# Eight products and no sums in the first pass of a seven-product kernel, with the first tiles placed between products

## The chip, the cores and the metric

The kernel runs on one core of a Trainium2 chip. The metric is the device time in microseconds (us). The engines are PE (TensorE: matmuls and transposes), DVE (VectorE), ACT (ScalarE), POOL (GpSimd) and SP (SyncE, which issues the DMAs here); each works through its own queue in order.

## The reference

Attention over chunks of 64 tokens, then two feed-forward layers, all in 32-bit floats:

```python
def _attn_ref(q, k, v):                       # q, k, v: (4, 8, 576, 64)
    ...
    scores = scale * np.matmul(q_c, k_c.transpose(0, 1, 2, 4, 3))
    scores = scores - np.max(scores, axis=-1, keepdims=True)
    attn = np.exp(scores)
    attn = attn / (np.sum(attn, axis=-1, keepdims=True) + 1e-09)
    out = np.matmul(attn, v_c)

def _moe_ref(x, w_in, w_out):                 # x: (2304, 512), w_in: (512, 2048)
    h = x @ w_in
    g = h * (1.0 / (1.0 + np.exp(-1.702 * h)))
    return g @ w_out

def _moe2_ref(x, w_in, w_out):
    h = x @ w_in
    sp = np.where(h > 20.0, h, np.log1p(np.exp(np.minimum(h, 20.0))))
    g = h * np.tanh(sp)
    return g @ w_out
```

The weights arrive as 64-bit floats.

## The kernel before

**Passes, blocks, steps.** Each layer's hidden dimension is cut in two, so there are four passes (n = 0 to 3; 0 and 1 are the first layer). A pass goes over five blocks of tokens: block 0 has 256 tokens, blocks 1 to 4 have 512 each; the order is 1, 0, 2, 3, 4 in the first three passes. A block has four steps (p = 0 to 3), each over two groups of 128 hidden rows. So there are 80 steps, numbered through: 0 to 3 are block 1 of the first pass, 4 to 7 block 0, 8 to 19 blocks 2 to 4; step 20 begins the second pass.

**A step** (`run`, from L539) makes the hidden rows of its two groups, applies the activation, and between its products runs the four `filler`s, which are the output products of the step before. Every value is kept as a high part (`fp32r`) and the rest, and a product of two values is three matmuls (`mm3`, L361); a product of one step's quarter is six matmuls of 256 columns (`prod`, L366). A *direct* step (`s.direct`) makes its 2 x 2 quarters with eight such products, in `half(h, c)`. The other steps make them with seven products of sums: four operands of weights (`S1` to `S4`, built by `Weights.add`) and four of tokens (`T1` to `T4`, built by `sums_of_tokens`); the running product X is copied out three times by ACT (`snap`, L611, L616, L622), and DVE adds three times (L617, L626, L638). In such a step the activation of the second half (L639) is asked for at the end of the step. `parts_before` makes high part and rest of that half (L381, L89) in the next step. Direct before the change are block 0 of every pass, and block 1 of the first pass. Steps before `FREE` write only to the PSUM banks x and y; from then on every second step uses a0 and a1.

**Preparation of operands.** `split` casts a quarter of tokens to a high part (ACT, L243) and subtracts for the rest (DVE); a seven-product block needs seven such splits, a direct one four. The buffers have names (`tag`) from B11 to T4. A weight piece (`pieces0`) arrives as pairs of 32-bit words; `convert` does scale (ACT, L130), join (DVE, L136 and L137), cast (ACT, L155) and rest (DVE, or POOL for the output weights). In the first pass the sums of weights come last: `sums_of_first` rebuilds the weights from their parts (L166, POOL and DVE) and adds, in steps 4 to 7.

**Attention** works on 18 tiles of 128 tokens (`Attention`). A tile is: two transposes (q, k) with a copy each by ACT, scores (L301), maximum and difference on DVE, exp on ACT, sums on DVE, normalising on POOL (L326), a transpose (L334) with a copy by ACT, and two products with the values (L347) with copies by DVE. Tiles 0 and 1 come before step 0, tiles 2 and 3 in `second_half`, which step 0 runs after its first two products. The others are cut into *ticks* (`ticks_of`), spread over the steps by `done` (27 of them in steps 0 to 3, all within steps 0 to 14). Each step has nine places (`place(0)` to `place(8)`) at which generators that have begun go on by one piece (`go_on`), and new ones begin. What is emitted there stands in that order in every engine's queue.

## Time and profile before

| | us |
|---|---|
| median of 3 runs | 938.03 (937.55 to 938.88) |
| the profiled execution | 935.45 |
| its span | 933.7 |
| PE busy | 871.1 (93%) |
| DVE busy | 589.6 (63%) |
| ACT busy | 398.4 (43%) |
| POOL busy | 71.8 (8%) |

All times of the trace are of the profiled execution, in us from the start of its span. Busy time of PE has modelled ends: consecutive matmuls overlap, and what one costs is read from start to start. The granted clock is a share of 2.4 GHz; 0.5 is 1.2 GHz. The steps start at: 0: 23.68, 1: 63.91, 2: 83.80, 3: 99.40, 4: 116.74, 7: 149.46, 8: 167.73, 9: 184.99, 15: 281.85, 19: 324.16, 20: 336.41.

### The profile page before, as it was taken

The page shows a single profiled execution, that of the slowest core. Times are in us where ns is not written, and L with a number is a line of the kernel's source. Part 1 is how long each engine was busy: PE and PEld are TensorE (multiplying, and loading weights), DVE is VectorE, ACT ScalarE, POOL GpSimd, SP SyncE. Part 2 cuts the span into 40 slices and gives each one's busy share as a digit, 9 for nine tenths or more (in the row PEclk, how much of TensorE's full clock was granted, in tenths as well). Part 3 has the DMA queues.
Part 4 walks back from the last instruction along what each step waited for, and adds up shares of the span by engine and source line. Part 5 has one row for each costly group of instructions (what it writes and reads, how often), then busy time and mean ns, then how long its engine had stood idle before and what let it go on. Part 6 is the DMA issues. An engine that isn't in the chain of part 4 may idle for free.

```text
span 933.7 us, 16021 instructions
## 1 busy us (share of the span) xinstructions
PE 871.1 (93%) x6318; PEld 776.9 (83%) x6318; DVE 589.6 (63%) x1121; ACT 398.4 (43%) x799; POOL 71.8 (8%) x60
## 2 busy tenths in 40 slices
PE   6679997789989988999999999999999999999998
PEld 4567777777879877998999989889999889999987
DVE  4456567546557888867767876545556785546442
ACT  3356564544545464443435444323243553323220
POOL 1011221000000111000000021000001110000000
PEclk9769998999999999999999999999999999999999
DMA  9464543233236667786767531210204242030202
GB/s 226 154 152 119 119 114 80 62 64 91 58 114 240 212 216 270 242 298 220 237 220 252 176 119 40 91 68 1 91 26 156 81 146 102 34 113 1 92 18 73
DMA packets 112491, 121.10 MB, mean 130 GB/s; under 512 B 60960, under 2 KB 80928, under 8 KB 110368
## 3 DMA queue, kind: packets, MB, share of 16 engines
q1 hardware_dynamic: 112416, 120.08, 41.2%
q8 instruction: 49, 0.80, 0.3%
q14 instruction: 26, 0.21, 0.1%
HBM read 83.89 MB, written 36.18 MB: 129 GB/s over the span
## 4 chain that ended last, share of the span: by engine, by line
PE 50%; DVE 4%; DMA 2%; ACT 1%; issue 1%; SPq 0%; ACTq 0%; DVEq 0%
PE acc L416 7%; PE acc L417 7%; PE acc L418 7%; PE x L362 4%; PE x L364 4%; PE x L363 4%; PE y L364 3%; PE y L363 3%; PE y L362 3%; PE acc L362 2%; PE acc L363 2%; PE acc L364 2%; DMA raw2o<-in_moe_w_out_dram 1%; DMA raw2i<-in_moe_w_in_dram 0%; DVE T1p L89 0%
## 5 line engine op out<-in xcount | busy, mean ns | idle before, releaser
L362 PE MATMUL acc<-gh,wo 128*128 128x512 f32 (+1 forms) x320 | 123.5, 386 | 0.0
L363 PE MATMUL acc<-gl,wo 128*128 128x512 f32 (+1 forms) x320 | 119.2, 372 | 0.0
L364 PE MATMUL acc<-gh,wo 128*128 128x512 f32 (+1 forms) x320 | 118.1, 369 | 0.0
L416 PE MATMUL acc<-wo,gh 128*128 128x512 f32 x288 | 113.8, 395 | 0.0
L417 PE MATMUL acc<-wo,gh 128*128 128x512 f32 x288 | 113.7, 395 | 0.0
L418 PE MATMUL acc<-wo,gl 128*128 128x512 f32 x288 | 112.0, 389 | 0.0
L381 DVE CAST gh<-t 128x512 fp32r<-128x512 f32 (+1 forms) x160 | 68.9, 430 | 67.9 <-ACT t L639 34.6
L89 DVE TENSOR_TENSOR gl<-t,gh 128x512 fp32r<-128x512 f32 (+1 forms) x160 | 105.7, 661 | 6.3
L639 ACT ACTIVATE t<-t 128x512 f32<-128x512 f32 x60 | 37.9, 632 | 130.3 <-DVE t L638 130.3
L364 PEld LDWEIGHTS acc<-gh,wo 128*128 128x128 f32 x320 | 60.5, 189 | 11.1
L362 PEld LDWEIGHTS acc<-gh,wo 128*128 128x128 f32 x320 | 60.9, 190 | 7.6
L363 PEld LDWEIGHTS acc<-gl,wo 128*128 128x128 f32 x320 | 60.9, 190 | 5.4
L418 PEld LDWEIGHTS acc<-wo,gl 128*128 128x128 f32 x288 | 54.1, 188 | 12.3
L416 PEld LDWEIGHTS acc<-wo,gh 128*128 128x128 f32 x288 | 54.6, 190 | 7.0
L417 PEld LDWEIGHTS acc<-wo,gh 128*128 128x128 f32 x288 | 54.7, 190 | 6.1
L626 DVE TENSOR_TENSOR t<-y,snap 128x256 f32<-128x256 f32 x60 | 25.3, 422 | 50.4 <-ACT snap L622 50.1
L616 ACT COPY snap<-x 128x256 f32<-128x256 f32 x60 | 22.3, 372 | 77.8 <-PE x L364 77.8
L622 ACT COPY snap<-x 128x256 f32<-128x256 f32 x60 | 22.3, 372 | 74.2 <-PE x L364 74.0
L301 PE MATMUL sc<-kt,qt 64*64 64x64 f32 x576 | 23.7, 240 | 22.5 <-ACT kt L290 20.4
L362 PE MATMUL x<-T2p,ws 128*128 128x256 f32 x120 | 35.4, 295 | 9.3 <-ACT snap L611 9.2
L301 PEld LDWEIGHTS sc<-kt,qt 64*64 64x64 f32 x576 | 21.1, 152 | 27.1 <-ACT kt L290 24.0
L632 ACT ACTIVATE t<-x 128x256 f32<-128x256 f32 x60 | 23.0, 383 | 47.6 <-PE x L364 47.5
(715 smaller groups left out, 2403.2 us busy)
## 6 DMA issues: line engine op xcount, KB each, us to landing
x<-x SPq DMA_DIRECT2D x16, 1024.0 KB, 6.1
part<-ps SPq DMA_DIRECT2D x34, 256.0 KB, 2.4
pl<-part SPq DMA_DIRECT2D x34, 256.0 KB, 4.4
out_dram<-pl SPq DMA_DIRECT2D x18, 256.0 KB, 2.1
v<-in_v_dram SPq DMA_DIRECT2D x16, 256.0 KB, 5.3
raw1i<-in_moe_w_in_dram SPq DMA_DIRECT2D x8, 512.0 KB, 5.2
raw1o<-in_moe_w_out_dram SPq DMA_DIRECT2D x8, 512.0 KB, 4.3
raw2i<-in_moe_w_in_dram SPq DMA_DIRECT2D x8, 512.0 KB, 4.4
```

The source lines that it names most:

```text
L89: eng.tensor_tensor(out=o, in0=a, in1=b, op=ALU.subtract)
L301: nc.tensor.matmul(pt[rs, o : o + CH], self.qt[rs, c0 : c0 + CH], self.kt[rs, c0 : c0 + CH], start=True, stop=True,)
L362: nc.tensor.matmul(o, wh, mh, start=start, stop=False, skip_group_check=more)
L363: nc.tensor.matmul(o, wh, ml, start=False, stop=False, skip_group_check=more)
L364: nc.tensor.matmul(o, wl, mh, start=False, stop=stop, skip_group_check=more)
L381: vec(gh[s, f][:, :n], t[:, :n])
L416: nc.tensor.matmul(o, a[:, ts], wh, start=start, stop=False)
L417: nc.tensor.matmul(o, a[:, ts], wl, start=False, stop=False)
L418: nc.tensor.matmul(o, b[:, ts], wh, start=False, stop=stop)
L626: nc.vector.tensor_add(tb[:, HB:], Y, snap[2])
L632: nc.scalar.activation(ta[:, HB:], X, func)
L639: nc.scalar.activation(tb, tb, func)
```

## The change

All blocks of the first pass are direct: eight products a step, no `snap`, no sums of tokens, no sums of weights (`rebuild` and `sums_of_first` go). The tokens of blocks 0, 2, 3 and 4 are split when half a block and the whole block have come (`TWO`, `MORE`, with buffers that are free then). The seven parts for the first seven-product block, in step 20, are made in step 19 (`AFTER_PASS`). `second_half` gets the products as its argument: tile 2's transposes and scores come ahead of the first product, tile 3's ahead of the second; weight pieces 2 to 4 are converted in it. Step 0 has no ticks any more; the ticks are spread over steps 1 to 15, 21 of them in steps 1 to 3, and `FREE` is 16. `load_next` loads one piece at each conversion, and pieces from 11 on use the first pieces' rooms again. In a seven-product step the activation of the second half is asked for in the next step (`act_before`), behind the first snapshot (or, in a direct step, behind the first half-product), and `parts_before` stands behind the first addition.

```diff
@@ -159,13 +160,6 @@
             both = self.parts[kind, f]
             sub(eng, both[:, 1], self.f32[kind, f], both[:, 0].bitcast(F32))
 
-        def rebuild(self, kind, f, eng):
-
-            t = wf32.tile([P, DM], F32, tag="wf", name=f"wr{self.n}{kind}{f}")
-            both = self.parts[kind, f].bitcast(F32)
-            eng.tensor_tensor(out=t, in0=both[:, 0], in1=both[:, 1], op=ALU.add)
-            self.f32[kind, f] = t
-
         def add(self, p):
 
             a, b = self.f32["i", 2 * p], self.f32["i", 2 * p + 1]
@@ -373,7 +367,7 @@
             mm3(o, wh[:, ws], wl[:, ws], mh, ml, start and kk == 0, stop and kk == 1, more)
 
     gh, gl = {}, {}
-    func = [AF.Gelu_apprx_sigmoid, AF.Mish]
+    func_of = lambda s: (AF.Gelu_apprx_sigmoid, AF.Mish)[s.m]
 
     def parts_of_g(s, f, t, n):
         gh[s, f] = gp.tile([P, 2 * HB], F32R, tag="gh", name=f"gh{s}{f}")
@@ -386,7 +380,7 @@
 
         def __init__(self, s, n, j, p):
             self.s, self.n, self.m, self.j, self.p = s, n, n // 2, j, p
-            self.direct = j == 0 or (n == 0 and j == 1)
+            self.direct = j == 0 or n == 0
             self.cols = size[j]
 
         def fillers(self):
@@ -485,7 +479,7 @@
         live, shifted = {}, []
         EARLY, SLOTS = 4, 8
 
-        FREE = 15
+        FREE = 16
 
         def go_on():
             for todo in list(going):
@@ -544,7 +538,7 @@
 
         def run(s, prev, jobs, middle=None):
 
-            p, w, func = s.p, W[s.n], (AF.Gelu_apprx_sigmoid, AF.Mish)[s.m]
+            p, w, func = s.p, W[s.n], func_of(s)
             fill = prev.fillers() if prev else [lambda: None] * 4
             n = s.cols
             tx, ty = ("a0", "a1") if s.s >= FREE and s.s % 2 else ("x", "y")
@@ -564,6 +558,11 @@
                         begin(todo())
                     del queue[:k]
 
+            def act_before():
+                for _, _, t, n in pending:
+                    nc.scalar.activation(t[:, :n], t[:, :n], func_of(prev))
+                exps()
+
             def parts_before():
                 while pending:
                     parts_of_g(*pending.pop(0))
@@ -578,13 +577,14 @@
                     prod(oc, w.operand(p, f"A{h + 1}2"), rhs[c][1], False, True)
 
                 if middle:
-                    half(0, 0)
-                    half(1, 0)
-                    middle()
+                    middle(half)
                 for h in range(2):
                     for c in range(1 if middle else 0, len(rhs)):
                         half(h, c)
-                        parts_before()
+                        if (h, c) == (0, 0):
+                            if prev and not prev.direct:
+                                act_before()
+                            parts_before()
                         place(4 * h + c)
                     t = tp.tile([P, 2 * HB], F32, tag=f"t{h}", name=f"t{s.s}{h}")
                     filler(2 * h)
@@ -610,11 +610,13 @@
                 prod(V, w.operand(p, "A12"), "B21")
                 act(snap[0], X)
                 prod(Y, w.operand(p, "S3"), "T3")
-                parts_before()
+                if prev and not prev.direct:
+                    act_before()
                 place(0)
                 prod(X, w.operand(p, "S2"), "T2", start=False, more=True)
                 act(snap[1], X)
                 nc.vector.tensor_add(ta[:, :HB], V, snap[0])
+                parts_before()
                 place(1)
                 filler(0)
                 place(2)
@@ -636,8 +638,6 @@
                 place(7)
                 filler(3)
                 nc.vector.tensor_add(tb[:, :HB], Y, snap[1])
-                nc.scalar.activation(tb, tb, func)
-                exps()
                 pending.append((s.s, 1, tb, n))
                 place(8)
             for h in range(2):
@@ -646,21 +646,26 @@
 
 
         w0 = W[0]
-        spare = []
-        for i in range(4):
-            t = wres.tile([P, 2, DM, 2], I32, tag=f"ws{i}", name=f"early{i}")
-            spare += [t[:, 0], t[:, 1]]
+        def early():
+
+            while True:
+                for i in range(4):
+                    t = wres.tile([P, 2, DM, 2], I32, tag=f"ws{i}", name=f"early{i}")
+                    yield t[:, 0]
+                    yield t[:, 1]
+
+        spare = early()
         pieces0 = [("i", 0), ("i", 1)]
         for p in range(NQ):
             if p + 1 < NQ:
                 pieces0 += [("i", 2 * p + 2), ("i", 2 * p + 3)]
             pieces0 += [("o", 2 * p), ("o", 2 * p + 1)]
-        loading, loaded = iter(pieces0), [0]
+        loading = iter(enumerate(pieces0))
 
         def load_next():
-            if (key := next(loading, None)) is not None:
-                w0.load(*key, room=spare.pop(0) if spare else None)
-                loaded[0] += 1
+            c, key = next(loading, (0, None))
+            if key:
+                w0.load(*key, room=next(spare) if c < 8 or c > 10 else None)
 
         for i in range(EARLY):
             live[i] = Attention(i)
@@ -717,22 +722,38 @@
         for f in range(2):
             w0.drop("i", f)
 
-        def second_half():
-
-            for a in (a2, a3):
-                whole(a.turn("q", "a0", act))
-                whole(a.turn("k", "a1", act))
-                whole(a.scores("o0" if a is a2 else "o1"))
-                a.exp()
-                a.sums(nc.gpsimd)
+        def second_half(half):
+
+            whole(a2.turn("q", "a0", act))
+            whole(a2.turn("k", "a1", act))
+            whole(a2.scores("o0"))
+            begin(convert(2))
+            half(0, 0)
+            a2.exp()
+            go_on()
+            whole(a3.turn("q", "a0", act))
+            whole(a3.turn("k", "a1", act))
+            whole(a3.scores("o1"))
+            a2.sums(nc.gpsimd)
+            begin(convert(3))
+            go_on()
+            half(1, 0)
+            a3.exp()
+            go_on()
+            whole(a2.turn_e("a0", act))
+            a3.sums(nc.gpsimd)
             tile_of(4)
-            whole(a2.turn_e("a0", act))
-            whole(a3.turn_e("a1", act))
+            go_on()
             whole(a2.values(0, "o2", vec))
             whole(a2.values(1, "o3", vec))
+            go_on()
+            begin(convert(4))
+            whole(a3.turn_e("a1", act))
+            go_on()
             whole(a3.values(0, "a0", vec))
-            whole(a3.values(1, "a1", vec))
+            whole(a3.values(1, "o0", vec))
             split_now(1, {"B12": "T1", "B22": None}, cols)
+            go_on()
             keep(0, 1)
 
         def convert(c):
@@ -741,19 +762,12 @@
             w0.scale(kind, f)
             yield
             w0.join(kind, f)
-            while loaded[0] < min(c + 7, len(pieces0)) and (loaded[0] < 11 or loaded[0] - 3 <= c):
-                load_next()
+            load_next()
             yield
             w0.cast(kind, f)
             yield
             w0.rest(kind, f, nc.vector if kind == "i" else nc.gpsimd)
             w0.drop(kind, f)
-
-        def sums_of_first(p):
-            w0.rebuild("i", 2 * p, nc.gpsimd)
-            w0.rebuild("i", 2 * p + 1, nc.vector)
-            yield
-            yield from w0.add(p)
 
         def rooms(kind, w, p):
 
@@ -810,35 +824,34 @@
                 source[c] = quarter(xs[0, j], c)
                 yield from split(c, to, tag)
 
-        marks = []
+
+        TWO = {0: {"B11": "T2", "B21": "T3"}, 2: {"B11": "T4", "B21": "B11"}}
+        TWO |= {3: {"B11": "B22", "B21": "T2"}, 4: {"B11": None, "B21": None}}
+        MORE = {2: {"B12": "B21", "B22": "T1"}, 3: {"B12": "T3", "B22": "T4"}}
+        MORE |= {4: {"B12": "T1", "B22": None}}
         for i in range(EARLY, NTILE + 1):
             ticks += ticks_of(i)
-            if i == 6:
-                ticks.append(lambda: now(lambda: keep(0, 0)))
-                ticks.append(lambda: splits(0, {"B11": "T2", "B21": "T3"}, fresh))
-            elif i == 8:
-                ticks.append(lambda: splits(2, {"B11": None, "B21": None}, fresh))
-            elif i > 8 and i % 4 == 2:
-                j = place(i - 1)[0]
+            j, t = place(i - 1)
+            if t == 1 and j != 1:
+                ticks.append(lambda j=j: splits(j, TWO[j], fresh))
+            if t == 3 and j != 1:
+                ticks.append(lambda j=j: splits(j, MORE[j], fresh))
+            if (t + 1) * P == size[j] and j != 1:
                 ticks.append(lambda j=j: now(lambda: keep(0, j)))
-                ticks.append(lambda j=j: sums_of_tokens(0, j))
-                ticks += [lambda: now(lambda: None)] * 3
-                if i == 10:
-                    ticks += [lambda c=c: split(c, fresh) for c in ("B22", "T1", "T4")]
-                marks.append(len(ticks))
-
-        half = marks[0] * 5 // 9
-        done = [half * i // 4 for i in range(4)]
-        for a, b, n in ((half, marks[0], 3), (marks[0], marks[1], 4), (marks[1], marks[2], 4)):
-            done += [a + (b - a) * i // n for i in range(n)]
-        done.append(marks[2])
+            if i == 10:
+                mark = len(ticks)
+
+        done = [0, 0] + [21 * i // 3 for i in range(1, 4)]
+        for a, b, n in ((21, mark, 4), (mark, (mark + len(ticks)) // 2, 4), ((mark + len(ticks)) // 2, len(ticks), 4)):
+            done += [a + (b - a) * i // n for i in range(1, n + 1)]
 
 
         FULL = {(3, 1): "B11", (3, 2): "B21", (3, 3): "T3", (3, 4): "T2", (3, 6): "T1", (3, 8): "B22"}
         LATE = {1: "T4"}
         AFTER_FIRST = {(1, 0): "B11", (1, 4): "B21", (2, 0): "T1", (2, 3): "B22", (2, 6): "T4"}
         AFTER_FIRST |= {(3, 5): "T3", (3, 6): "T2"}
-        AFTER_TICKS = {(3, 5): "T3", (3, 6): "T2"}
+        AFTER_PASS = {(3, 0): "T3", (3, 1): "T2", (3, 2): "T4", (3, 4): "B11", (3, 5): "B21"}
+        AFTER_PASS |= {(3, 6): "T1", (3, 8): "B22"}
         TO_FIRST = {(3, 2): "B21", (3, 3): "B11"}
 
         fresh = {}
@@ -856,7 +869,7 @@
             if s.p == 0:
                 cols.update(fresh)
                 fresh.clear()
-                if not s.direct and blocks[b - 1].j:
+                if not s.direct and not blocks[b - 1].direct:
                     for i, c in LATE.items():
                         jobs.setdefault(i, []).append(lambda c=c: split(c, cols))
             if nxt and nxt.n > 0:
@@ -868,12 +881,12 @@
                     jobs.setdefault(2, []).append(lambda m=nxt.m, j=nxt.j: sums_of_tokens(m, j))
                 if nxt.j == 0 and s.p == 3:
                     source.update({c: quarter(xs[nxt.m, 0], c) for c in ("B11", "B21")})
-            if nxt and (nxt.n, nxt.j) != (0, 0):
+            if nxt and nxt.n:
                 table, tags = FULL, {}
                 if nxt.j == 0:
                     table, tags = TO_FIRST, {"B11": "T2", "B21": "T3"}
-                elif s.j == 0:
-                    table = AFTER_TICKS if s.n == 0 else AFTER_FIRST
+                elif s.direct:
+                    table = AFTER_FIRST if s.n else AFTER_PASS
                 for (p, i), c in table.items():
                     if p == s.p:
                         jobs.setdefault(i, []).append(
@@ -882,10 +895,9 @@
 
             if s.n == 0:
                 if here < 4:
-                    lo = 2 + 4 * here
-                    todo += [lambda c=c: convert(c) for c in range(lo, min(lo + 4, len(pieces0)))]
-                if 4 <= here < 8:
-                    todo.append(lambda p=here - 4: sums_of_first(p))
+                    lo = (5, 6, 10, 14)[here]
+                    hi = (6, 10, 14, 16)[here]
+                    todo += [lambda c=c: convert(c) for c in range(lo, hi)]
             if s.n < 3:
                 todo += change_of(W[s.n + 1], here - per)
             if s.n:
```

## Rows read from the trace of the kernel before

**Rows 1.** The page, part 1: busy us and share of the span.
```profile
PE 871.1 (93%) x6318; PEld 776.9 (83%) x6318; DVE 589.6 (63%) x1121; ACT 398.4 (43%) x799; POOL 71.8 (8%) x60
```

**Rows 2.** Windows: length, busy PE, PEld, DVE, ACT, POOL, granted clock, DMA share, GB/s.
```profile
23.68:63.91 40.23, 25.20 (x281) 22.47 (x281) 18.39 (x34) 16.30 (x27) 4.40 (x4) 0.71 0.65 174
63.91:336.41 272.50, 246.03 (x2186) 217.40 (x2185) 177.75 (x346) 144.25 (x250) 32.94 (x27) 0.97 0.41 115
336.41:933.70 597.29, 584.12 (x3673) 526.17 (x3671) 382.47 (x722) 229.38 (x508) 31.70 (x21) 1.00 0.38 130
...
83.80:99.40 15.60, 15.13 (x148) 13.08 (x146) 10.73 (x21) 11.69 (x18) 3.81 (x3) 1.00 0.48 148
149.46:167.73 18.27, 12.61 (x131) 12.02 (x129) 12.38 (x28) 8.47 (x16) 2.52 (x2) 0.81 0.25 49
281.85:292.41 10.56, 10.56 (x68) 9.53 (x66) 9.06 (x18) 6.00 (x13) 0.00 (x0) 1.00 0.59 204
336.41:348.75 12.34, 10.81 (x67) 9.58 (x66) 10.60 (x21) 6.23 (x14) 1.30 (x1) 1.00 0.76 256
```

**Rows 3.** Waits of PE, steps 1 to 19: us, times, longest.
```profile
PE sc L301 <- ACT kt L290: 10.9, 8, 4.5
PE pv L347 <- ACT a L338: 8.5, 8, 1.3
```

**Rows 4.** Waits of PE, step 0.
```profile
PE sc L301 <- ACT kt L290: 9.5, 4, 5.8
```

**Rows 5.** Waits of PE, step 20 to the end.
```profile
PE x L362 <- ACT snap L611: 6.7, 7, 1.6
```

**Rows 6.** Timeline of PE: start, duration, instruction; every sixth matmul.
```profile
65.35 0.41 PE L362 MATMUL h1x<-B21p,wi 128*128 128x256 f32 x1
...
66.63 0.41 PE L362 MATMUL h1x<-B12p,wi 128*128 128x256 f32 x1
...
281.85 0.28 PE L362 MATMUL x<-B11p,wi 128*128 128x256 f32 x1
...
282.56 0.28 PE L362 MATMUL y<-B21p,wi 128*128 128x256 f32 x1
```

**Rows 7.** Groups in steps 1 to 19: count | busy us, mean ns | idle before.
```profile
L626 DVE TENSOR_TENSOR t<-y,snap 128x256 f32<-128x256 f32 x12 | 5.0, 421 | 6.0 <-ACT snap L622 5.9
L616 ACT COPY snap<-x 128x256 f32<-128x256 f32 x12 | 4.5, 372 | 11.1 <-PE x L364 11.1
L183 ACT CAST ws<-s 128x512 fp32r<-128x512 f32 x12 | 7.4, 618 | 15.3 <-DVE s L89 15.3
L89 DVE TENSOR_TENSOR T2s<-x,T1s 128x512 f32<-128x512 f32 x4 | 2.7, 686 | 0.0
```

**Rows 8.** Timeline of ACT in step 7; brackets: idle before, releaser.
```profile
156.23 0.62 ACT L183 CAST ws<-s 128x512 fp32r<-128x512 f32 x1 [0.43 <-DVE s L89]
...
157.23 0.59 ACT L290 COPY kt<-trk 128x512 f32<-128x512 f32 x1
```

**Rows 9.** Timeline of step 0: tile 3's scores, the last token part's cast.
```profile
34.63 1.15 PE L301 MATMUL sc<-kt,qt 64*64 64x64 f32 x32 [2.12 <-ACT kt L290]
...
44.15 0.62 ACT L243 CAST B12p<-x 128x512 fp32r<-128x512 f32 x1 [2.41 <-DVE x L358]
```

**Rows 10.** Groups over the span: scores, and four transposes for each tile.
```profile
L301 PE MATMUL sc<-kt,qt 64*64 64x64 f32 x576 | 23.7, 240 | 22.5 <-ACT kt L290 20.4 <-ACT e L318 1.2 <-DVE kt L290 0.9
...
L334 PE MATMUL at<-ident,e 128*128 128x128 f32 x72 | 11.9, 291 | 9.4 <-POOL e L326 9.4
```

**Rows 11.** Timeline of ACT in step 20.
```profile
338.79 0.63 ACT L639 ACTIVATE t<-t 128x512 f32<-128x512 f32 x1 [3.81 <-DVE t L638]
```

**Rows 12.** Timeline of step 0: joins on DVE and a product on POOL.
```profile
54.79 0.69 DVE L137 SCALAR_TENSOR_TENSOR wf0i<-early 128x512 int32<-128x512 int32 x1
...
59.23 1.04 POOL L326 TENSOR_TENSOR e<-e,rc 128x512 f32<-128x512 f32 x1 [18.82 <-DVE rc L325]
59.38 1.43 DVE L137 SCALAR_TENSOR_TENSOR wf0o<-early 128x512 int32<-128x512 int32 x1
```

## The prediction

> **What bounds the kernel now.** First the page's engine line: TensorE is busy for 93% of the span [rows 1], so the question is where the other 7% lies. The windows view answers it [rows 2]. I cut the trace at the starts of steps (a step's first product is found in PE's timeline): 23.68 us is step 0, 63.91 step 1, 336.41 step 20, where the second pass begins. From 336.41 to the end PE is busy for 584.1 of 597.3 us. A step that waits for nothing takes 10.56 us and PE fills it (281.85 to 292.41). In steps 1 to 19 PE is busy for 246.0 of 272.5 us, so 26.5 us are idle; in step 0 it is busy for 25.2 of 40.2 us, at a mean granted clock of 0.71. So the loss sits in the first pass, in steps 0 to 14, which also carry attention.
>
> What ends those waits is read from the waits of PE [rows 3, 4]. In step 0 it is above all ScalarE's copy of kt (9.5 us in four waits). In steps 1 to 19 it is the copies of kt (10.9 us) and a (8.5 us), both short ScalarE copies in a strict queue. The timeline shows what stands ahead of them: the longest wait, 4.5 us, ended with the kt copy at 157.23 us, and the instruction two places ahead of it was a cast of the weights' sums, which had waited for VectorE [rows 8]. Step 7 (149.46 to 167.73) has VectorE busy for 12.4 of 18.3 us while PE is busy for 12.6 only [rows 2]: VectorE was building the sums for the seven-product steps. PE also slows down there: the granted clock of that stretch is 0.81.
>
> **The change, term by term.** The sum is made against the profiled execution, 935.45 us with a span of 933.7. The median of the runs, 938.03, lies 2.6 us above it, and I add that at the end.
>
> Term C, the products. Six matmuls of 256 columns, one product, take 0.71 us at 2.4 GHz (281.85 to 282.56) [rows 6]. Steps 8 to 19 get eight products for seven: 12 x 0.71 = 8.5 us more on PE, the bound engine, with nothing to hide it.
>
> What leaves the other engines, with the durations of [rows 7]: the three snapshots (0.37 us of ScalarE each) and three additions (0.42 us of VectorE each) of twelve steps; four token sums (0.69 us each) of three blocks, and three of their seven splits (about 0.62 us on ScalarE and 0.69 on VectorE each); and for four weight pairs one rebuild and two differences on VectorE (of the shape of a token sum, 0.69 us), four half-width additions (0.42 us) and two casts of 0.62 us. VectorE: 36 x 0.42 + 12 x 0.69 + 9 x 0.69 + 4 x (3 x 0.69 + 4 x 0.42) = 45 us of the 178 that it works in steps 1 to 19 [rows 2]. ScalarE: 36 x 0.37 + 9 x 0.62 + 8 x 0.62 = 24 of 144 us. None of it lay on PE, so its price is nothing but the waits that it causes, which is term B.
>
> Term B, waits in steps 1 to 19. Idle 26.5 us; and stretches at 1.2 GHz cost about 6.5 us more: a product takes 1.28 us there instead of 0.71 (65.35 to 66.63) [rows 6], and this holds in step 1 and after the long waits of steps 7 and 8 (granted 0.81 in step 7). Together 33 us. What stays: a chain of transpose, copy, next matmul needs about 1 us on ScalarE, and it shows wherever two attention pieces have less PE work than that between them. In the seven-product steps some places have one product (0.71 us) between them; in the eight-product steps two products or half an output group, about 1.4 us, which covers such a copy. Steps 4 to 7 are narrow (256 columns) and now carry attention in all four, with some places that have nothing between them: I leave 1.5 us each. For steps 1 to 3 and 8 to 15 I leave 0.8 us each, which 83.80 to 99.40 us with 0.5 us idle [rows 2] supports. That makes 15 us: gain 18 us. Ends: 6 us (only the waits in and around steps 7 to 9 go) and 24 us.
>
> Term A, step 0. Before, both first products run at 23.68, then tiles 2 and 3 go through attention alone, one latency after another: tile 3's scores start at 34.63, and the cast of the last token part starts at 44.15 [rows 9], 9.5 us later. Now a product stands between tile 2's and tile 3's scores and one after them, and the conversions of i2, i3 and o0 start there, not in the steps behind. The products give way to tile 2's transposes, which can run while PE waits for the first token split. I estimate tile 3's scores at 31 to 34 us, so that the last parts are there at 41 to 44 and step 1 starts, after 24 more matmuls at either clock (2.9 or 5.1 us), at 46.5 to 52. I take 49.5: step 0 takes 25.8 us instead of 40.2. The attention ticks that step 0 held (transposes and scores of tiles 4 and 5) move into later steps: 2 x (1.3 + 2 x 0.66) = 5 us of PE [rows 10]. Net gain 9.4 us, ends 5 and 13. The DMA queue is moved past too: piece loads 8 to 10 and tile 4's loads now follow the conversions instead of the whole middle, and the transfers are about 65% of the engines' time in step 0 [rows 2], so I see no new wait; if tile 4 lands late, step 1's first transposes stall PE, within the ends.
>
> Two rules speak against this term. First, step 0's granted clock is 0.71 [rows 2]. The Trainium skill, "TensorE: Matmul & The Clock Gate", Part 1, says that the array's clock is at half unless sustained work releases it; short products between latencies would then all run at half. By that rule alone, 48 matmuls at 213 instead of 119 ns make 4.5 us, where I count about half of it. Second, the join of a weight piece took 1.43 us beside a GpSimd product that began at 59.23, and the one at 54.79 took 0.69 [rows 12]. The Trainium skill, "SBUF — State Buffer", section "SBUF: two separate sides", says that a VectorE operation with two SBUF inputs and a GpSimd one exclude each other. Three joins now stand near tile 2's and 3's GpSimd products; by the rule that takes up to 2.2 us off this term.
>
> Term D, activations asked for later. In passes 2 to 4 PE waited 6.7 us in seven steps for the first snapshot [rows 5]. In the first of them ScalarE's queue stood idle 3.81 us for VectorE's last addition, before the activation, with the snapshot behind it [rows 11]. Now snapshot one goes first; the activation then stands ahead of snapshot two, which is needed about 2 us later, so a wait up to 1.6 us is covered. Nobody needs the activated half until the third output group. VectorE is busy 10.6 of 12.3 us in step 20 [rows 2], so a little may come back as another wait. I take 6.5 us, with the pipeline's refilling counted in; ends 2 and 9. Moving bank use from step 15 to 16, the token buffers' new tags and the seven splits in step 19 instead of six I cost at nothing: PE has 4 us of work between the last use of the first buffer and step 20, and VectorE is then lighter by the sums; without that cover it is about 1.5 us in step 20.
>
> Sum: 935.45 + 8.5 - 18 - 9.4 - 6.5 = 910.0; with 2.6 for the median, 912.6 us.
>
> **The rivals.** (1) The waits are attention's own latency, not VectorE's backlog: kt and a copies wait 19.4 us [rows 3], and most of that returns with each tile. Then B is 10 and D 4: 938 + 8.5 - 10 - 9.4 - 4 = 923 us. For it: single waits of about 1 us recur in steps 9 to 13, where no weight sums run. Against: the largest lie with the sums. (2) Everything fits better: B 24, D 9: 938 + 8.5 - 24 - 10.5 - 9 = 903. (3) Step 0 isn't shorter: PE takes its queue in order, so each product waits behind a score that waits for ScalarE, all at 1.2 GHz; A is 0 or less, since the conversions lengthen the same queues: 922. (4) Slower: the deferred activation holds snapshots two and three. It stands in ScalarE's queue behind nothing but VectorE's addition; if that comes over 4 us into the step in every step, the third product waits in each of the 48 seven-product steps. From 0.55 us a step it eats the whole gain of 25 us; at 0.8 it gives 951. Against it: after 336 us VectorE works 382 of 597 us [rows 2], and the backlog is in a few steps. (5) The parts cancel: 938.
>
> **How the numbers follow.** Forecast 0.53, (1) 0.19, (2) 0.12, (3) 0.08, (4) 0.05, (5) 0.03. The likeliest is 912.6. Summing all good ends gives about 900, all bad ends 933; both at once is unlikely, and the rivals at 903, 922 and 923 must be in: 899 to 930. A measurement of this kernel can tell about 0.2% from no change. Faster 0.92, same 0.03, slower 0.05.
>
> **What would show it.** Step 1 starting at 46 to 52 us, step 20 at 311 to 325 (336.4 before), under 17 us of PE idle between; no ws casts in the first pass; no PE wait for the first snapshot after it, and steps of 10.6 to 11 us from 20 to 22. Wrong if the kt and a copies still hold PE for over 15 us in steps 1 to 15, if step 1 starts after 56 us, or if a new wait for the second snapshot or a token part shows.

## The result and the profile after

The changed kernel takes 914.21 us (median of 4, 910.98 to 916.33) where the kernel before took 937.87 in the same comparison: a ratio of 0.974, with a 95% interval of 0.971 to 0.977. The forecast was 912.6 us, from 899 to 930. The profiled execution is the fastest of the four, 910.98 us, with a span of 909.2 us against 933.7.

The page of the changed kernel: engines (busy us, share), and busy tenths and granted clock in 40 slices.

```profile
PE 873.0 (96%) x6390; PEld 780.7 (86%) x6390; DVE 544.4 (60%) x1036; ACT 374.2 (41%) x734; POOL 69.8 (8%) x56
PE   7689999999999999999999999999999999999998
PEclk9889989999999999999999999999999999999999
```

PE does 72 matmuls more than in [rows 1] and is busy for 96% of the span instead of 93%; VectorE has 45 us less to do and ScalarE 24, as counted in the prediction. What is still open lies in the first slices. The windows of the changed kernel, with the columns of [rows 2]: step 0, steps 1 to 19, step 20 to the end, then steps 8, 20, 21 and 22.

```profile
26.06:47.94 21.88, 14.82 (x164) 13.06 (x161) 13.68 (x27) 9.22 (x15) 3.62 (x3) 0.77 0.79 224
47.94:318.00 270.06, 256.55 (x2339) 227.47 (x2337) 140.76 (x270) 129.26 (x196) 30.15 (x24) 0.98 0.44 120
318.00:909.20 591.20, 583.36 (x3673) 527.08 (x3671) 377.17 (x718) 225.22 (x505) 33.22 (x21) 1.00 0.39 131
146.44:162.14 15.70, 13.01 (x150) 12.16 (x149) 6.66 (x14) 7.54 (x13) 1.05 (x1) 1.00 0.56 135
318.00:328.56 10.56, 10.56 (x68) 9.53 (x66) 8.93 (x19) 5.70 (x12) 1.35 (x1) 1.00 0.99 322
328.56:340.75 12.19, 11.08 (x68) 9.36 (x67) 9.92 (x17) 5.97 (x14) 2.77 (x2) 1.00 0.66 232
340.75:352.23 11.48, 10.81 (x67) 9.59 (x66) 10.20 (x20) 5.77 (x12) 1.30 (x1) 1.00 0.87 303
```

Against [rows 2] this gives the account by stage. Step 1 starts 15.97 us earlier (47.94 for 63.91). Steps 1 to 19 are 2.44 us shorter although they carry twelve products and two tiles' ticks more. The rest is 6.09 us shorter. Together 24.5 us.

The waits of PE in the changed kernel (us in total, times, longest): steps 1 to 19, then step 20 to the end.

```profile
PE pv L341 <- ACT a L332: 6.7, 5, 2.0
PE sc L295 <- ACT kt L284: 4.6, 3, 3.2
```

```profile
PE x L356 <- ACT snap L617: 0.8, 1, 0.8
PE x L356 <- ACT snap L611: 0.7, 1, 0.7
```

In steps 1 to 19 the copies of kt and a hold PE for 11.3 us instead of the 19.4 of [rows 3]. From step 20 on the first snapshot holds it for 0.7 us instead of the 6.7 of [rows 5]; the token part T3p holds it for 1.3 us, where it was 1.1 before.

What the remaining waits stand behind is in ScalarE's queue. Its timeline in step 1, ahead of the longest wait (PE stood for 3.24 us, until 64.48):

```profile
59.56 1.28 ACT L312 ACT_TABLE_LOAD   x1
60.86 0.63 ACT L312 ACTIVATE e<-e 128x512 f32<-128x512 f32 x1
61.40 0.65 ACT L131 ACTIVATE raw0o<-raw0o 128x512 f32<-128x512 f32 x1
62.06 1.28 ACT L591 ACT_TABLE_LOAD   x1
63.35 0.60 ACT L591 ACTIVATE t<-h1y 128x512 f32<-128x512 f32 x1
63.85 0.58 ACT L284 COPY kt<-trk 128x512 f32<-128x512 f32 x1
```

The kt copy takes 0.58 us and follows 4.3 us of other work, of which 2.6 are two loads of function tables: one for attention's exp, one to go back to the layer's activation. The prediction named casts of sums as what stood there [rows 8]; with the casts gone, the loads are what is left. Four more waits, for the a copy, are alike: a load for the exp starts 2.45 us before PE goes on (at 117.97, 160.01, 191.74 and 239.61).

### The profile page after: what moved, and what is told of

Same layout as the page of the kernel before. It is cut to its first block, busy times and chain, and to the rows that moved or that the text cites. A ratio compares the mean times of both kernels' runs of the same rounds, so it can differ in the third digit from the quotient of the medians.

```text
span 909.2 us, 15978 instructions
## 1 busy us (share of the span) xinstructions
PE 873.0 (96%) x6390; PEld 780.7 (86%) x6390; DVE 544.4 (60%) x1036; ACT 374.2 (41%) x734; POOL 69.8 (8%) x56
## 4 chain that ended last, share of the span: by engine, by line
PE 56%; DMA 2%; DVE 1%; ACT 0%; issue 0%; SPq 0%; DVEq 0%; ACTq 0%
PE acc L410 7%; PE acc L411 7%; PE acc L412 7%; PE x L358 5%; PE x L357 5%; PE x L356 5%; PE y L357 4%; PE y L358 3%; PE y L356 3%; PE acc L356 3%; PE acc L357 3%; PE acc L358 3%; DMA raw2i<-in_moe_w_in_dram 1%; DMA raw2o<-in_moe_w_out_dram 0%; DVE pl L449 0%
## 5 line engine op out<-in xcount | busy, mean ns | idle before, releaser
L611 ACT COPY snap<-x 128x256 f32<-128x256 f32 x48 | 17.9, 373 | 134.7 <-PE x L358 134.7
L618 DVE TENSOR_TENSOR t<-y,snap 128x256 f32<-128x256 f32 x48 | 20.3, 423 | 87.9 <-PE y L358 52.3
L352 DVE COPY x<-pv 128x256 f32<-128x256 f32 x34 | 14.3, 424 | 53.5 <-PE pv L341 53.3
L617 ACT COPY snap<-x 128x256 f32<-128x256 f32 x48 | 17.9, 374 | 51.7 <-PE x L358 51.7
L624 ACT COPY snap<-x 128x256 f32<-128x256 f32 x48 | 17.9, 373 | 49.7 <-PE x L358 49.6
L628 DVE TENSOR_TENSOR t<-y,snap 128x256 f32<-128x256 f32 x48 | 20.2, 421 | 27.1 <-ACT snap L624 27.1
L320 POOL TENSOR_TENSOR e<-e,rc 128x512 f32<-128x512 f32 x18 | 20.1, 1117 | 203.5 <-DVE rc L319 109.2
L341 PEld LDWEIGHTS pv<-a,v 64*64 64x64 f32 x576 | 20.2, 149 | 16.8 <-ACT a L332 11.7
```

Source lines behind the costliest of these rows:

```text
L320: eng.tensor_tensor(out=self.eg, in0=self.eg, in1=rc.to_broadcast([P, G, CH]), op=ALU.mult)
L341: nc.tensor.matmul(pt[r * D : (r + 1) * D, p * CH : (p + 1) * CH], self.v[cs, h * D : (h + 1) * D], self.a[cs, p * P + r * CH : p * P + (r ...
L618: nc.vector.tensor_add(ta[:, :HB], V, snap[0])
L628: nc.vector.tensor_add(tb[:, HB:], Y, snap[2])
```

## The experiments

The theory: short ScalarE copies stand in a strict queue behind work of VectorE and ScalarE that is not itself on the path (the weights' sums above all), and that is where terms B and D come from; term A comes from products placed between the latencies of tiles 2 and 3. The rivals: the waits are attention's own latency and return whatever else runs; step 0 gains from moved work, not from the interleaving; the later activation does nothing that a lighter VectorE would not.

**The change once more.** The changed kernel, unaltered, beside the next three.

> The changed kernel once more, as the mark for the runs beside it. Its first four times went from 911.0 to 916.3 us with the granted clock going from 0.984 to 0.975, so I expect a median of 912 to 916 us and the longer times at the lower clock.

914.12 us (909.38 to 916.31), ratio 0.974 (0.972 to 0.977). The profiled execution, 914.12 us, is longer above all in steps 8 and 9 (windows):

```profile
148.01:165.24 17.23, 14.54 (x151) 13.50 (x149) 6.66 (x14) 8.35 (x14) 1.04 (x1) 0.89 0.53 129
165.24:182.22 16.98, 16.98 (x150) 15.00 (x149) 6.03 (x13) 6.44 (x10) 1.04 (x1) 0.91 0.32 74
```

In the other trace the same steps took 15.70 and 15.61 us at a granted clock of 1.00. The work is the same, and PE waits for the same 2.69 us in step 8; the clock fell once and once it did not. These two steps are 2.9 us longer here. Step 1 also starts 1.5 us later (49.43), and steps 28 and 29 are 2.3 us shorter. So a spread of 5 to 7 us belongs to this kernel, and a difference of 3 us between two single profiles proves nothing.

**The later activation alone**, on the kernel before:

```diff
 ...
 prod(Y, w.operand(p, "S3"), "T3")
-parts_before()
+if prev and not prev.direct:
+    act_before()
 ...
 act(snap[1], X)
 nc.vector.tensor_add(ta[:, :HB], V, snap[0])
+parts_before()
 ...
 nc.vector.tensor_add(tb[:, :HB], Y, snap[1])
-nc.scalar.activation(tb, tb, func)
 exps()
```

> The kernel before with one part of the change: the second half's activation is asked for in the next step, behind the first snapshot (and its parts behind the first addition). Theory (the order of ScalarE's queue makes term D): the 9.2 us that PE waited for the first snapshot over the span go, most of them without a new wait: 929 to 933 us against 937.9. Rival (the waits come from VectorE's load; the order only moves them to the second snapshot or to the last addition): 936 to 938 us.

929.82 us (925.54 to 930.64), ratio 0.990 (0.988 to 0.992). Its passes 2 to 4 (window), and PE's waits there:

```profile
334.74:927.70 592.96, 582.67 (x3673) 525.66 (x3671) 379.73 (x723) 225.94 (x507) 33.62 (x21) 1.00 0.38 131
```

```profile
PE x L362 <- ACT snap L623: 2.9, 3, 2.1
PE x L362 <- ACT snap L617: 0.7, 1, 0.7
```

4.3 us of the 597.3 go there, and 1.7 in the first pass, whose steps 8 to 19 still have snapshots. The wait for the first snapshot fell from 6.7 to 0.7 us, and a new one of 2.9 us came for the second: the rival, that the waits only move to the second snapshot, is right for that part.

**The change without it**, the same edit undone on the changed kernel:

> The changed kernel without that part: the activation is asked for at the end of the step, as before. Theory: the waits for the first snapshot return from step 21 on, about 5 to 6.5 us: 919 to 921 us. Rival (the lighter VectorE in steps 16 to 19 has already removed them): within 2 us of the changed kernel, 913 to 916 us.

918.01 us (913.53 to 920.34), ratio 0.979 (0.976 to 0.981), 3.9 us over the run beside it; the two intervals just touch. That lies between the two expectations, 919 to 921 and 913 to 916. Its passes 2 to 4, and the waits:

```profile
317.93:911.70 593.77, 583.48 (x3673) 526.09 (x3671) 379.70 (x718) 227.82 (x505) 31.69 (x21) 1.00 0.38 130
```

```profile
PE x L356 <- ACT snap L608: 3.4, 5, 1.6
PE x L356 <- ACT snap L613: 1.8, 2, 1.4
```

So without any deferral these passes are already 3.5 us shorter than before, and the first snapshot's wait is half of [rows 5]. Step 20 gives 1.8 of it (10.56 us for 12.34). There the reason is seen in ScalarE's queue: step 19 is a direct step now, so no activation that waits for an addition of VectorE [rows 11] stands ahead of step 20's first snapshot. Step 19's last activation begins at 315.43, the snapshot at 318.84, and that waits for PE alone. The rival named a lighter VectorE in steps 16 to 19, but it is hardly lighter: it is busy for 34.4 of 45.0 us in these four steps, against 36.4 of 44.0 before. Where the other 1.7 us come from is not shown. Term D has two causes, the deferral and the direct step 19.

**Products behind the tiles**, as before the change, all else as changed:

```diff
 def second_half(half):
+    half(0, 0)
+    half(1, 0)
 ...
     begin(convert(2))
-    half(0, 0)
 ...
-    half(1, 0)
     a3.exp()
```

> The changed kernel with the first two products ahead of tiles 2 and 3 again, and all else as changed (conversions in the middle, no ticks in step 0). Theory (the interleaving shortens the middle): tile 3's scores and the last token part come 3 to 5 us later, so step 1 starts at 51 to 53 us instead of 47.9 and the time is 916 to 919 us. Rival (term A comes from the ticks that left step 0 and the conversions that moved, not from the order of products): within 1.5 us of the changed kernel.

917.35 us (915.34 to 919.55), ratio 0.978 (0.976 to 0.981): 3.2 us more. Step 1 starts at 53.77, against 47.94 and 49.43 in the two traces of the change. Tile 3's scores and the last token part's cast in this kernel, then in the changed one:

```profile
35.14 1.45 PE L295 MATMUL sc<-kt,qt 64*64 64x64 f32 x32 [2.12 <-ACT kt L284]
...
48.02 0.62 ACT L237 CAST B12p<-x 128x512 fp32r<-128x512 f32 x1 [2.17 <-DVE x L352]
```

```profile
29.40 1.15 PE L295 MATMUL sc<-kt,qt 64*64 64x64 f32 x32 [0.78 <-ACT kt L284]
...
41.99 0.62 ACT L237 CAST B12p<-x 128x512 fp32r<-128x512 f32 x1 [2.17 <-DVE x L352]
```

With the products between, tile 3 is 5.7 us earlier and the last cast 6.0; step 1 gets 4.3 to 5.8 of it. But without them 53.77 is still 10 us ahead of the kernel before, of which the prediction's 5 us of PE work is only moved to later steps. So the interleaving is about half of term A. For the other half, look behind the last cast: from it to step 1 were 19.8 us before (44.15 to 63.91) and are 5.8 here (48.02 to 53.77). Before, the ticks of tiles 4 and 5 stood there, with waits for kt of 0.9 and 5.8 us, and the conversions, whose three joins in step 0 began at 46.54, 54.79 and 59.38. Here these three joins begin at 33.90, 39.55 and 44.71, in the middle, and the last cast comes 3.9 us later than before. No run parts the ticks from the conversions.

**The weights' sums, made for nothing** in steps 4 to 7 of the changed kernel:

```diff
+def rebuild(self, kind, f, eng):
+    t = wf32.tile([P, DM], F32, tag="wf", name=f"wr{self.n}{kind}{f}")
+    both = self.parts[kind, f].bitcast(F32)
+    eng.tensor_tensor(out=t, in0=both[:, 0], in1=both[:, 1], op=ALU.add)
+    self.f32[kind, f] = t
 ...
+def sums_of_first(p):
+    w0.rebuild("i", 2 * p, nc.gpsimd)
+    w0.rebuild("i", 2 * p + 1, nc.vector)
+    yield
+    yield from w0.add(p)
 ...
+if s.n == 0 and 4 <= here < 8:
+    todo.append(lambda p=here - 4: sums_of_first(p))
```

> The changed kernel (eight products everywhere in the first pass) with the weights' sums of the first pass made again in steps 4 to 7, for nothing: about 16 us of VectorE, 5 of ScalarE, 5 of GpSimd. Theory (VectorE's backlog held the kt and a copies): 4 to 8 us longer, with waits of several us in steps 4 to 9. Rival (attention's own latency): within 2 us of the changed kernel.

930.10 us (928.11 to 931.77), ratio 0.992 (0.990 to 0.993): 16 us more. Steps 5 and 8 (windows), and PE's waits from 115 to 182 us:

```profile
115.14:131.79 16.65, 12.72 (x97) 12.03 (x93) 9.03 (x22) 7.67 (x12) 0.00 (x0) 0.69 0.55 126
160.60:181.41 20.81, 16.00 (x150) 14.87 (x148) 10.72 (x21) 8.77 (x15) 1.27 (x1) 0.84 0.42 102
```

```profile
PE pv L348 <- issue: 8.1, 2, 5.4
PE pv L348 <- ACT a L339: 5.9, 2, 3.9
PE sc L302 <- ACT kt L291: 2.6, 1, 2.6
```

Nobody reads these sums, yet PE waits for attention's a and kt copies, at a clock of 0.69 and 0.84. Steps 5 to 8 take 66.3 us instead of 48.8. ScalarE's queue ahead of the longest of these waits (3.9 us), and VectorE's last instruction before the longest wait put down to "issue":

```profile
118.03 0.62 ACT L184 CAST ws<-s 128x512 fp32r<-128x512 f32 x1 [1.91 <-DVE s L90]
...
121.29 0.58 ACT L339 COPY a<-at 128x512 f32<-128x512 f32 x1
```

```profile
153.80 0.69 DVE L90 TENSOR_TENSOR e<-sc,mx 128x512 f32<-128x512 f32 x1
...
154.59 1.12 PE L348 MATMUL pv<-a,v 64*64 64x64 f32 x16 [5.40 <-issue]
```

The a copy stands behind a cast that waited for VectorE's sums, and between the two there are the layer's activation, a table load, the exp and a second cast. For the 8.1 us put down to "issue" the trace names no releaser, but the program does: the product with the values writes bank a0, in which the next tile's scores lie until VectorE has taken their maximum and their difference. In both places PE goes on 0.1 us after that difference has ended (139.19 and 154.49). So VectorE's backlog holds PE directly too, and not through ScalarE alone. The rival, at most 2 us, falls, and the theory's 4 to 8 was too little.

**All the removed work for nothing**: the same, with the token sums, and each step's PSUM copies and additions.

> As the run before, and also the token sums, the extra three splits and the three snapshots and additions of each step of blocks 2 to 4, all for nothing: the 45 us of VectorE and 24 of ScalarE are back, while PE makes eight products. Theory: term B is lost again, 12 to 18 us longer than the changed kernel, 926 to 932 us. Rival: under 6 us longer.

977.22 us (975.40 to 982.41), ratio 1.043 (1.040 to 1.046), where 926 to 932 were expected. Inconclusive, because the experiment made waits that the kernel before did not have, 31 us in all; the largest:

```profile
PE h17a L363 <- DVE dead L592: 5.0, 2, 4.1
```

The idle additions read the PSUM bank that the next product writes, and products waited for them.

**The rest for nothing, from SBUF**: token sums, splits and per-step additions of that size, without the weights' sums, and without touching the products' banks:

```diff
+def dead_step(h, c):
+    if s.n or s.j < 2 or (h, c) == (1, 1):
+        return
+    d = sp.tile([P, HB], F32, tag=f"s{2 * h + c}", name=f"dead{s.s}{h}{c}")
+    xq = xs[0, s.j][:, 2 * h + c, :HB]
+    act(d, xq)
+    nc.vector.tensor_add(d, xq, d)
 ...
```

(the token sums and splits, `dead_tokens`, are left out here).

> The changed kernel with the other part of the removed work made for nothing: in blocks 2 to 4 of the first pass the token sums, three splits' worth of cast and difference, and in each step three copies on ScalarE and three additions on VectorE of the snapshots' size, all from SBUF, so that none waits for a product: 29 us of VectorE and 19 of ScalarE, while PE makes eight products. If VectorE's and ScalarE's load in steps 8 to 19 held PE back too: 5 to 10 us longer than the changed kernel (914). If the harm came from the weights' sums in steps 4 to 8 alone: within 2 us of it.

920.61 us (916.98 to 921.68), ratio 0.981 (0.979 to 0.983): 6.5 us more. Steps 13 and 14 are 1.9 and 2.2 us longer, and step 20 takes 14.25 us for 10.56, with a wait that the change did not have:

```profile
PE x L357 <- DVE B11p L90: 1.9, 1, 1.9
```

**One product less** in each step of blocks 2 to 4 of the first pass; the output lacks that term.

```diff
+less = s.n == 0 and s.j >= 2 and (h, c) == (1, 1)
+prod(oc, w.operand(p, f"A{h + 1}1"), rhs[c][0], True, less)
+if less:
+    return
```

> The changed kernel without one product (six matmuls) in each step of blocks 2 to 4 of the first pass, so that these steps have seven; the output lacks that term. If PE is the bound there (term C stands in full): 8.5 us shorter, 905 to 906 us. Rival (steps 8 to 15 are bound by attention's chain, so the eighth product was half hidden): 3 to 6 us shorter.

907.42 us (906.37 to 910.22), ratio 0.968 (0.966 to 0.970): 6.8 us less, between the two expectations (8.5, and 3 to 6). Steps 10 to 19:

```profile
179.11:312.17 133.06, 128.96 (x1077) 113.06 (x1076) 74.08 (x138) 59.63 (x92) 11.58 (x9) 1.00 0.48 147
```

In the changed kernel they take 140.25 us (177.75 to 318.00): 7.19 us more for ten products, 0.72 each, and each step gives about that (0.69 to 0.75). Step 20 takes 11.56 us for 10.56, so 1 us comes back.

**No change of table**: the exp of tiles 4 to 17 replaced by the layer's own activation, so that the attention weights are not the reference's.

```diff
-nc.scalar.activation(self.eg, self.eg, AF.Exp, scale=scale)
+f = AF.Exp if self.i < 4 else AF.Gelu_apprx_sigmoid
+nc.scalar.activation(self.eg, self.eg, f, scale=scale)
```

> The changed kernel with the softmax's exp of tiles 4 to 17 replaced by the step's own activation function, so that ScalarE never loads another table there; the attention weights are not the reference's. Theory (what is left of PE's waits in steps 1 to 15, 13 us, stands behind two table loads of 1.28 us per tile): 8 to 13 us shorter, 901 to 906 us. Rival (the waits are the chain transpose, copy, matmul itself): under 3 us shorter.

895.14 us (894.48 to 897.35), ratio 0.955 (0.954 to 0.957): 19 us less, where 8 to 13 were expected. Steps 1 to 19:

```profile
48.11:302.89 254.78, 251.67 (x2338) 223.31 (x2337) 142.67 (x270) 92.59 (x168) 30.32 (x24) 1.00 0.47 127
```

PE has the same matmuls, 3.1 us idle instead of 13.5, and 4.9 us less busy time for them at a clock of 1.00. That is 15.3 us against the first trace of the change and 18.2 against the second, whose steps 8 and 9 ran slower.

**The activation by tanh**, which is the same function: 1 / (1 + exp(-1.702 h)) is (1 + tanh(0.851 h)) / 2. ScalarE makes the tanh, VectorE multiplies, and the half goes into the making of the parts. Steps 0 to 15.

```diff
-nc.scalar.activation(t[:, :n], o[h][:, :n], func)
+nc.scalar.activation(t[:, :n], o[h][:, :n], AF.Tanh, scale=0.851)
 ...
+nc.vector.scalar_tensor_tensor(
+    t[:, :n], t[:, :n], 1.0, o[h][:, :n], op0=ALU.add, op1=ALU.mult)
 ...
-vec(gh[s, f][:, :n], t[:, :n])
+nc.vector.tensor_scalar(gh[s, f][:, :n], t[:, :n], 0.5, None, op0=ALU.mult)
 ...
```

> The changed kernel with the same function in the first sixteen steps by another way: h times (1 + tanh(0.851 h)) / 2. By the Trainium skill, ScalarE: Activation LUTs, section Table sets: the hidden batching unit, exp and tanh are of one table set, so the two table loads a tile should go, as in the run that used one function for both (895.1 us); VectorE gets one operation of about 0.7 us more for each half, 22 us in the first pass. Theory (table loads ahead of the kt and a copies are what is left of PE's waits): 896 to 902 us. Rival (VectorE's extra work brings the waits back): 908 to 916 us.

898.21 us (897.58 to 899.01), ratio 0.958 (0.957 to 0.960): 16 us less than the change. Table loads as groups (count, busy us, mean ns, idle before), in the changed kernel:

```profile
L591 ACT ACT_TABLE_LOAD x15 | 19.2, 1283 | 23.5 <-PE h11x L358 6.1 <-issue 3.5 <-PE h15y L358 3.1
L312 ACT ACT_TABLE_LOAD x14 | 18.0, 1283 | 0.3
```

With two single ones more they are 31, 40 us of ScalarE; by tanh there are 3. Steps 1 to 19 by tanh, and PE's waits in them:

```profile
50.01:306.39 256.38, 251.73 (x2339) 223.29 (x2337) 159.86 (x302) 93.81 (x169) 30.00 (x24) 1.00 0.46 126
```

```profile
PE sc L295 <- ACT kt L284: 2.4, 3, 1.2
PE pv L341 <- ACT a L332: 1.6, 3, 0.7
```

The Trainium skill, "ScalarE: Activation LUTs", section "Table sets: the hidden batching unit", says that tables come in named sets, that exp and tanh share one, and that calls are to be grouped by set; the 3 loads agree. Its section "What ACT_TABLE_LOAD costs" gives 1283 ns for the load, as here, and about 2.66 us for a whole switch. The timeline of step 1 above shows exp starting at 60.86, 0.02 us after its load ended, and the copy ahead of the load had ended at 59.55, 0.01 us before it began. So no more than the load is seen between the instructions here.

**PE kept busy in the middle**: 29 matmuls on zeros into a free bank, in step 0's waits.

```diff
 a3.exp()
 go_on()
+keep_warm(12, 2, "o1")
 whole(a2.turn_e("a0", act))
+keep_warm(4, 3, "o1")
```

(and 4, 3 and 6 more in the same way further down).

> The changed kernel with 29 matmuls on zeros in the waits of PE in the middle of step 0 (34 to 43 us), so that the clock may stay at 2.4 GHz. Theory (the clock falls in those waits, and that it falls at another moment in each execution makes the spread of 909 to 916 us): at33 to 46 us the granted clock stays near 1.0, step 1 starts 1 to 3 us earlier, 909 to 912 us with a spread under 3 us. Rival (the spread comes from elsewhere, the matmuls only delay the chain): 914 to 917 us with the same spread.

912.63 us (907.72 to 914.35), ratio 0.973 (0.970 to 0.975): 1.5 us less, which this comparison doesn't tell from nothing. Two stretches of step 0, from 36 to 42 us, in the changed kernel, then in this one:

```profile
36.00:39.00 3.00, 1.89 (x36) 1.55 (x36) 2.76 (x8) 0.59 (x1) 1.23 (x1) 0.67 0.85 231
39.00:42.00 3.00, 1.81 (x33) 1.43 (x32) 0.96 (x3) 0.59 (x2) 0.00 (x0) 0.50 0.12 38
```

```profile
36.00:39.00 3.00, 2.45 (x43) 1.60 (x40) 2.86 (x6) 1.69 (x3) 0.51 (x2) 1.00 0.62 184
39.00:42.00 3.00, 2.52 (x37) 1.47 (x36) 2.13 (x5) 0.58 (x1) 1.15 (x1) 1.00 0.02 5
```

The clock stays at 2.4 GHz, and step 1 starts at 47.31 us. But the five executions spread over 6.6 us, where under 3 were expected: the clock in step 0 is not what makes the spread of this kernel. Steps 8 and 9 took 17.15 and 17.07 us in this trace, at a granted clock of 0.90.

**Both**, tanh and the matmuls on zeros:

> Both of the last two together: no table loads in the first sixteen steps, and 29 matmuls on zeros in PE's waits in the middle of step 0. In the run with the zeros alone the granted clock stayed at 1.00 from 33 to 50 us, against 0.50 to 0.67 from 36 to 48 without them, but steps 8 and 9, behind a wait of 2.0 us for a table load, ran partly at 1.2 GHz in the profiled execution and took the gain. Theory (the clock falls wherever PE waits long enough, and each such place has to be closed): with both closed step 1 starts at 47 to 48 us instead of 50.0, 895 to 897 us. Rival (the zeros give nothing): 898 to 899 us.

896.21 us (895.75 to 897.77), ratio 0.957 (0.956 to 0.958). It is the lowest median of a kernel that computes the whole reference; its interval overlaps that of tanh alone, so what the zeros add there (2 us by the medians) is not settled.

## Why the prediction was right

By its own terms, from the profiled spans, with both traces of the change:

| term | forecast (ends) | measured | second trace |
|---|---|---|---|
| C, products | +8.5 | +8.6 | +8.6 |
| B, waits in steps 1 to 19 | -18 (-6 to -24) | -16.0 | -13.1 |
| A, step 0, net of moved ticks | -9.4 (-5 to -13) | -11.0 | -9.5 |
| D, activation later | -6.5 (-2 to -9) | -6.1 | -7.4 |
| sum | -25.4 | -24.5 | -21.4 |

C is 12 times the 0.72 us that one product cost in a step with one less. The others are worked out from the windows with the 5 us of moved ticks of the prediction, an estimate: A is 15.97 less 5, B is 2.44 and 5 and 8.6. B, A and D lie within their ends in both traces. That the sum came within 1 us in the first is in part luck: B fell 2.0 us short there and A gave 1.6 us more.

**Term C** holds: PE is the bound and nothing hides a product; each step of the experiment gave its whole 0.72 us, and 1 us of the sum came back in step 20.

**Term B** has the right size and the right cause for what went. The weights' sums alone, put back for nothing, cost 16 us; the other 30 us of VectorE's work in the count cost 6.5, and 3.7 of those in step 20. So rival 1, that most waits return with each tile, falls. The two together are more than the whole term: put back into the new order, the work costs more than it did in the old one, so these runs show the cause and not each part's share. What the new spread of the ticks gives was not tried by itself. What the step missed is what stays. I left 15 us as the latency of short chains. By the trace of the changed kernel it is 13.5 us idle and, against the 251.7 us that the same matmuls take at full clock, 4.9 us of slower matmuls; but it is not that latency. Without the change of tables only 3.1 us idle and none of the slower matmuls remain. I read what stood in front of the longest wait [rows 8] and took it for the whole; the 31 loads were in the trace of before too (14 for exp, 16 to go back, 1 at the start), and 19 us by the medians hung on 28 of them.

**Term A** came out 1.6 us better in the first trace and as forecast in the second, with its steps mixed up. Tile 3's scores start at 29.40 (31 to 34 forecast), step 1 at 47.94 (46.5 to 52 forecast). The interleaving, which the prediction put first, is worth 3 to 6 us of it; the rest comes from the ticks that left and from the conversions. The prediction says that the conversions moved into the middle of step 0 from "the steps behind"; but their three joins stood in step 0 before as well, at its end. Rival 3, that step 0 isn't shorter, falls.

The two rules that spoke against this term: on the clock, about half of the matmuls of step 0 ran at either level, as counted. The first 24 ran at a granted 1.00 (twelve in about 1.53 us). Of the last 24 all but the last five or six ran at 0.50; the clock had fallen at about 37 us, after waits of 2.2 and 1.0 us of PE in the attention of tiles 2 and 3. "All at half" by the rule alone does not hold here; and holding the clock up brought step 1 forward by 0.6 us against the one trace of the change and by 2.1 against the other. On the port, one join of a weight piece in the middle ran beside a GpSimd product:

```profile
28.03 0.69 DVE L138 SCALAR_TENSOR_TENSOR wf0i<-early 128x512 int32<-128x512 int32 x1
...
33.26 1.05 POOL L320 TENSOR_TENSOR e<-e,rc 128x512 f32<-128x512 f32 x1 [14.12 <-DVE rc L319]
33.52 1.34 DVE L138 SCALAR_TENSOR_TENSOR wf0i<-early 128x512 int32<-128x512 int32 x1
```

1.34 us beside it, 0.69 alone: this agrees with the rule ("SBUF — State Buffer" in the Trainium skill, as cited in the prediction), for one join of the three that I allowed for.

**Term D** is right in size, half right in cause: the later activation gives 2.6 to 4.3 us in these passes, and the rest of the change (the direct step 19 ahead of them, as far as is seen) 1.8 to 3.5, by which of the two is counted first. (Steps 28 and 29 wait behind a ScalarE instruction for which the next pass's weights must arrive. They take 22.2 us together before and after, but 19.8 in the second trace of the change, so 2 us of a difference between two traces can be theirs.) Step 20 takes 10.56 us, but steps 21 and 22 take 12.2 and 11.5, over the 10.6 to 11 that the prediction asked for. Part of that is the wait it named as a sign of error, for the second snapshot. ScalarE's timeline in step 21:

```profile
330.09 0.63 ACT L563 ACTIVATE t<-t 128x512 f32<-128x512 f32 x1 [0.19 <-DVE t L640]
332.82 0.59 ACT L445 COPY ps<-acc 128x512 f32<-128x512 f32 x1 [2.10 <-DMA part<-ps]
333.31 0.38 ACT L617 COPY snap<-x 128x256 f32<-128x256 f32 x1
```

The deferred activation, which rival 4 feared, is done at 330.7. The snapshot stands behind a copy of partial sums that waited 2.1 us for its buffer's DMA. It happens once, for 0.8 us here and 1.8 us in the second trace; rival 4 needed 0.55 us in each of 48 steps. The wait for a token part, the other sign that it named, is not new (T3p, 1.3 us for 1.1).

The 2.6 us for the median: this profile too is the fastest execution, 3.2 us below the median. I had taken that offset over from the kernel before, where the trace did not explain it, so that it fits is luck. Here the second trace, which is the median of its five, is 3.1 us longer, and steps 8 and 9 with their lower clock are 2.9 us longer in it.

## What to carry to other kernels

An engine that is off the path still sets the pace of PE when short copies that PE needs stand in its queue: 20 us of work (15 on VectorE, 5 on ScalarE, besides four sums on GpSimd) whose result nobody read cost 16 us. For each wait, list everything in the releasing engine's queue for the few us before it, for several waits and not the longest alone: a kind of instruction that comes in most of them, as the table loads here, is worth more than the largest single one. When a change shortens a stage in several ways, price the work that merely leaves the stage or moves within it apart from the clever new order; here each was about half.

## What the runs showed of the hardware

The time of one kernel spread over 5 us with its clock: in the four executions of the change 910.98, 913.93, 914.49 and 916.33 us go with granted clocks of 0.984, 0.979, 0.976 and 0.975 over the span. Behind the same waits in step 8 (0.69 and 2.00 us) the clock stayed at 1.00 in one trace and was 0.89 in the other. With the table loads gone, PE's longest wait in steps 1 to 19 is 1.2 us instead of 3.2, and the executions lie closer together: within 1.4 us by tanh (897.58 to 899.01), 2.0 us with the matmuls on zeros as well, and 2.9 us with the exp replaced. Why the clock fell in one execution and not in another stays open.
